# Edits in the opening of an attention and SwiGLU kernel: fill-in matmuls, a first fetch in halves, later stores, tied casts, and Down's scale noted later

## The chip, the cores and the metric

One core of a Trainium2 chip. The metric is the device time of one execution in microseconds (us), the median of several runs; lower is better. Engines are named as in the profile: PE is TensorE's matmuls and PEld its weight loads, DVE is VectorE, ACT is ScalarE, POOL is GpSimd, and SP is SyncE, which issues the DMAs in this kernel.

## The reference

For x of 2048 tokens by 512 features, xn is x normalized per token (layernorm without gain). The result is x + A(xn) * silu(B(xn)):

```
A: q, k, v = split(xn @ wqkv)            # 32 heads of 16
   p = softmax(where(0 <= i - j < 256, q k^T / 4, -1e9))
   A(xn) = (p v) @ wo
B: h = silu(xn @ w1) * (xn @ w3)         # 1792 wide
   B(xn) = h @ w2
```

## The kernel before

The tokens are worked in four tiles of 512, numbered t = 0 to 3. The FFN's width is cut in 14 blocks of 128. The large matmuls run in fp16: each operand is a high half and a low half (lo = value - hi), and a product is three matmuls of 512 columns, xh·wh, xh·wl and xl·wh, summed in PSUM. Weights are scaled by powers of two before they are cut in halves, and the scales are found on the chip: squares of each row (L249 on ACT, L251 on DVE), a cast of the sums to bf16 (L261, tile `sb`), a matmul with ones on PE (`powers`, L280 and L285), a short chain on DVE that makes the scale (L291 to L304), and then the cut (`split`: high half L333 on ACT, low half L334 on DVE; `split_pool`: L342 and L343 on ACT, L345 on POOL). In tile 0 the kernel does all this to the weights while it computes, and stores the cut weights in DRAM; tiles 1 to 3 load them from there.

The four pairs of columns of wqkv for q and k are called qk0 to qk3, one for each group of 8 heads; their raw halves are loaded at L395. `project` (L597, result read by L614 on ACT and L618 on DVE) computes q or k of a head group, `value` (L567, L570) computes v. Cut k and q of a group are stored in DRAM by L621 to L625, and `fetch` (L641) loads them back in the layout of the scores: `KA` the keys, `qa` the queries. Attention runs in two passes: scores for the row maxima (L665 on PE, L679 on DVE), then scores again, mask (L753), exponential (L756 on ACT) and values (L774).

`gate_up` (L1036) makes gate and up of a block, each in one bank: tanh of gate on ACT (L1051), times gate on DVE (L1055), times up on DVE (L1060), then the cut of h (L1069 on ACT, L339 on POOL). `measure(f)` finds the scales of blocks f and f + 1 of w1 and w3 and cuts them. `measure_down(k)` does it for groups of blocks of w2 (squares L923, cast L927), with the scale of the group in L935 to L945: `q` is the group's maximum, `dsc` what Down's result is multiplied with (L938), `fq` the running maximum over groups (L940, L942), `sw` the scale of the blocks (L945). Down is L1261 (and L1179 in folded form from tile 2 on), the output L1313 with its stores in L1324.

PSUM has two banks that alternate (`bank`, named m0 and m1 and shown as m), two tiles of two banks for scores (`scores_bank`, shown as s) and one (po) for scores and values. Matmuls that want bank m wait until the engine that reads its last content is done. SBUF has 54 slots, handed out by `take` and given back by `give(tile, after=n)`, n steps later.

PE runs its instructions in the order of the program text, which a planner for scores (`spread`, `more`, `beside_scores`) writes out. On the other engines a scheduler orders the instructions when the program is built, by readiness and priority; `tc.issue_after(ins)` keeps an instruction behind another of the same engine. `later(n, f)` runs f n steps further on in the program, where a step is one call of `step`, about once per piece of PE work. `lasts["emptied"]` is the last DVE instruction that read a bank of m.

In the opening, `keep_busy(n)` (L1534 to L1537) issues n matmuls of ones, whose results nobody reads, into a bank: 24 at the start, then 3, then 4 ahead of the first projections.

Of the kernel before, what the change touches and what calls it, by code (L numbers as in the profile page):

```python
# [10 lines left out]
F32 = mybir.dt.float32  # L11
# [4 lines left out]
ALU = mybir.AluOpType  # L16
# [5 lines left out]
P = 128  # L22
# [61 lines left out]
def tile_block(ctx: ExitStack, tc: tile.TileContext, x, wqkv, wo, w1, w3, w2, out):  # L84
# [59 lines left out]
    def later(n, f):  # L144
        made_so_far[0] += 1
        queue.append((now[0] + n, made_so_far[0], f))
# [16 lines left out]
    def bank(shape, dtype=F32):  # L163

        open_bank[0] = b = 1 - open_bank[0]
        return psm.tile(shape, dtype, name=f"m{b}", tag=f"m{b}", bufs=1)
# [414 lines left out]
    def project(t, g, k, terms=(range(3),), scores_bank=False):  # L581
# [7 lines left out]
        def part(n):  # L589
# [1 line left out]
            w = WQ[t, g, k]  # L591
            xh, xl = X[t]
            if n == 0:
                cell["pp"] = pss.tile([P, 2, TW], F32, name="s")[:, 0, :] if scores_bank else bank([P, TW])
            for c, i in parts[n]:
                a, b = ((0, xh), (1, xh), (0, xl))[i]
                nc.tensor.matmul(cell["pp"], w[:, (a * NC + c) * P:(a * NC + c + 1) * P], b[:, c, :], start=(c, i) == parts[0][0],  # L597
# [33 lines left out]
        WQ[t, g, k] = w = take(F16)  # L631
        nc.sync.dma_start(w, dWQ[g, k])

    def fetch(t, g):
        QA[t, g] = qa = qpool.tile([P, 4, TW], F16, name="qa")
        ka = keys(t, g)
        c0 = 0 if t else 2 * P
        for dst, d in ((ka[:, :, c0:], dK[g][:, :, t * TW - 2 * P + c0:(t + 1) * TW]),
                       (qa, dQ[g][:, :, t * TW:(t + 1) * TW])):
            for r in range(2):  # L640
                lasts["load"] = nc.sync.dma_start(dst[64 * r:64 * r + KR],  # L641
                                  d[64 * r:64 * r + 64].rearrange("(a d) i t -> (d i) a t", d=DH))

# [224 lines left out]

    measured = set()

    def measure(f, apart=0):

        raws = [RAW.pop(f + i) for i in range(2)]
        sb = squares([raws[0][0], raws[1][0], raws[0][1], raws[1][1]], on_act=4 if f > 2 else 2, apart=apart)

        def scale(s=None):
            pp = small.tile([P, 2, 2], F32, name="pp")
            pi = small.tile([P, 2, 2], F32, name="pi")  # L880
            return then(s, powers(sb, 4, pp.rearrange("p a b -> p (a b)"), pi.rearrange("p a b -> p (a b)"), s),
                        lambda: rest(pp, pi))

        def rest(pp, pi):
            ff = slice(f, f + 2)
            nc.vector.tensor_scalar(sg_scale[:, ff], pp[:, 0, :], 0.5 / (WS * XS), None, op0=ALU.mult)
            nc.vector.tensor_mul(p13[:, ff], pp[:, 0, :], pp[:, 1, :])
            measured.update((f, f + 1))

            def cut(i, k):  # L890
                if k == 0:
                    WF[0, f + i] = [[None, None], WF.pop((0, f + i), [None, None])[1]]
                WF[0, f + i][0][k] = a = take(F16)
                split_pool(a[:, 0:D], a[:, D:], raws[i][k], pi[:, k, i:i + 1])
                give(raws[i][k], after=5)
            for i in range(2):
                for k in range(2):
                    later(((1, 2, 4, 6) if f < 8 else (1, 5, 9, 13))[2 * i + k], lambda i=i, k=k: cut(i, k))
        if started:
            beside_scores(8, scale)  # L900
        else:
            later(10 if apart else 6, scale)

# [11 lines left out]
    def measure_down(k, f):  # L915
# [17 lines left out]
        def rest(p2):  # L933
# [1 line left out]
            nc.vector.tensor_mul(p2, p2, p13[:, f0:f1])  # L935
            q = small.tile([P, 1], F32, name="q")
            nc.vector.tensor_reduce(q, p2, axis=AX.X, op=ALU.max)
            nc.vector.tensor_scalar(down_scale[:, k:k + 1], q, 1.0 / (HS * WS), None, op0=ALU.mult)  # L938
            if k:
                nc.vector.tensor_max(fold_q, fold_q, q)  # L940
            else:
                nc.vector.tensor_copy(fold_q, q)  # L942
            nc.vector.reciprocal(q, q)
            sw = small.tile([P, 4], F32, name="sw2")
            nc.vector.tensor_scalar(sw[:, 0:n], p13[:, f0:f1], q, WS, op0=ALU.mult, op1=ALU.mult)  # L945

            def cut(f):
                raw = RAW2.pop(f)
# [344 lines left out]
    def total(t, b):  # L1293
# [4 lines left out]
        def part(half):  # L1298
# [16 lines left out]
            if half:  # L1315
# [10 lines left out]
                if t == NT - 1:  # L1326
                    store()
                else:
                    later(4, store)
                if b == 3:  # L1330
                    give(*(OT[t, g] for g in range(NG)))
        return opening([(6, lambda h=h: part(h)) for h in range(2)])
# [22 lines left out]
    def feed_forward():  # L1355
# [4 lines left out]
        for t in range(NT):  # L1360
            for f in range(FB):
                if t == 0:
# [3 lines left out]
                    elif f + LEAD == FB - 1:  # L1366
                        pieces += [(0, lambda f=f: load(0, f)) for f in range(FB - 2, FB)]
                    if f % 2 and f + 3 < FB:
                        pieces.append((0, lambda f=f + 3: later(5, lambda: measure(f, 1)) if f == 6 else measure(f, 1)))
                    pieces += [(0, lambda f=f: load_down(0, f)) for f in range(f + 2 if f else 0, min(f + 3, FB))]  # L1370
                    for m in range(f + 1 if f else 0, min(f + 2, FB)):
                        k = next(k for k, (_, f1) in enumerate(GROUPS) if m < f1)
# [158 lines left out]
        nc.gpsimd.memset(KA[2][:, a, :].bitcast(F32), TWO_ONES)  # L1531


    def keep_busy(n):  # L1534
        ps = bank([P, 4, P])
        for _ in range(n):
            nc.tensor.matmul(ps, onesb, onesb.unsqueeze(1).to_broadcast([P, 4, P]), start=True, stop=True)  # L1537

# [19 lines left out]
        flush()  # L1558
    with tc.issue_after(lasts["hi"].ins), tc.issue_after(lasts["x"].ins):
        qk[1][1]()  # L1560
    keep_busy(4)


    k00, q00 = (project(0, 0, k, ((0,), (1,), (2,)), k) for k in (1, 0))
    run([k00[0], q00[0], k00[1]])
    qk[1][2]()
    with tc.issue_after(lasts["scale"].ins):
# [2 lines left out]
    qk[1][3]()  # L1570
    with tc.issue_after(lasts["hi"].ins):
        run([k00[2], q00[2]])
    later(1, lambda: fetch(0, 0))
    k01 = project(0, 1, 1, ((0, 2), (1,)))
    run(k01[:1])
    wv[2]()
# [4 lines left out]
    sc["o"] = scaled(SQ["wv"][3], OS / WS, "so")  # L1581
    with tc.issue_after(lasts["hi"].ins):
        measure(0)
    run(project(0, 1, 0, scores_bank=True))
    later(1, lambda: fetch(0, 1))
    run(value(0, True))
    qk[2][1]()
# [35 lines left out]
    for n, u in enumerate(units):  # L1623
# [7 lines left out]
            wout[0]()  # L1631
        if n == 7:
            wout[1](2)
            beside_scores(12, lambda s: then(s, wout[2](s), lambda: later(2, lambda: wout[3](2)), lambda: later(3, out_scale)))
        want += a_unit - other[n]
        mine = more(want)

# [39 lines left out]
```

## Time and profile before

| quantity | before |
|---|---|
| median of 3 runs | 811.76 us (811.22 to 811.85) |
| profiled execution | 811.24 us |
| its span | 809.4 us |
| PE busy | 793.7 us (98%) |
| DVE, ACT, POOL busy | 631.2, 392.1, 377.1 us |
| granted TensorE clock | full in all 40 slices |

The profile covers one execution. Its page gives the busy time of each engine and the chain of work that ended last. In a timeline a row is the start, the duration, engine, line and operation, output and input tiles and the number of instructions put together; what stands in brackets is the idle time of that engine just before, and whose work ended it. A row with no bracket followed its predecessor with little or no idle time. Matmuls overlap: one of 512 columns is listed with 0.38 us, but in a row of them they start 0.216 us apart. 1.8 us of the profiled execution lie outside the span.

### The profile page before, as it was taken

To read this page: it belongs to the slowest core of one execution; us is meant where nothing else is said; L and a number is where in the kernel's file an instruction comes from. 1 tells how busy PE (TensorE), PEld (TensorE's weight loads), DVE (VectorE), ACT (ScalarE), POOL (GpSimd) and SP (SyncE) were. 2 spreads that over 40 slices of the span, in tenths; PEclk is the share of its full clock that TensorE was granted. 3 is DMA by queue.
4 is the path that set the end of the run, shared out by engine and by line. 5 is a ranking of instruction groups with operands and counts; after the bars stand their busy time and mean duration, and the time that the engine had idled before them with its cause. 6 is when DMAs were issued, how large, how long until landed. Compare 5 with 4: busy or idle time off the path is not lost.

```text
span 809.4 us, 23944 instructions
## 1 busy us (share of the span) xinstructions
PE 793.7 (98%) x9176; PEld 403.7 (50%) x9176; DVE 631.2 (78%) x2037; ACT 392.1 (48%) x591; POOL 377.1 (47%) x732
## 2 busy tenths in 40 slices
PE   8999989999999999999999999999999999999998
PEld 4444444444444444444444454456544754466465
DVE  8788788887888777887988888777778787875437
ACT  6879586553546544345344433344444234344411
POOL 2345376342329445354353455530346276550670
PEclk9999999999999999999999999999999999999999
DMA  9968554835576474757655634646372644335321
GB/s 282 265 214 267 160 183 134 278 114 191 160 199 208 134 232 139 218 142 263 160 162 181 194 104 119 185 137 179 105 201 74 160 139 137 113 90 172 111 65 62
DMA packets 109795, 134.19 MB, mean 166 GB/s; under 512 B 18864, under 2 KB 64880, under 8 KB 109680
## 3 DMA queue, kind: packets, MB, share of 16 engines
q1 hardware_dynamic: 109392, 132.13, 54.6%
q8 instruction: 72, 1.18, 0.6%
q10 hardware_dynamic: 288, 0.52, 0.2%
q14 instruction: 43, 0.35, 0.1%
HBM read 91.23 MB, written 36.57 MB: 158 GB/s over the span
## 4 chain that ended last, share of the span: by engine, by line
PE 79%; DVE 8%; ACT 6%; DMA 3%; issue 2%; SPq 1%; POOL 0%; ACTq 0%; DVEq 0%
PE m L1036 30%; PE po L774 8%; PE m L1261 8%; PE m L1179 8%; PE m L597 7%; PE s L746 5%; PE m L1313 4%; PE m L567 4%; PE s L665 3%; DMA slot<-in_B_w_dram 2%; DVE junk L679 2%; PE po L665 2%; ACT slot L342 1%; ACT pt L756 1%; ACT sqa L249 1%
## 5 line engine op out<-in xcount | busy, mean ns | idle before, releaser
L1036 PE MATMUL m<-XH,slot 128*128 128x512 f16 x896 | 267.4, 380 | 1.6 <-DVE slot L618 1.2
L756 ACT ACTIVATE pt<-s,es 128x1024 f32<-128x1024 f32 x152 | 167.5, 1112 | 193.7 <-DVE s L753 186.5
L1036 PEld LDWEIGHTS <-slot 128*128 128x128 f16 x1344 | 124.7, 98 | 156.0 <-issue 12.0
L1036 PE MATMUL m<-XL,slot 128*128 128x512 f16 x448 | 169.9, 379 | 0.0
L753 DVE TENSOR_TENSOR s<-s,MK 128x256 f32<-128x256 f32 (+2 forms) x280 | 118.7, 434 | 51.2 <-PE s L746 47.0
L679 DVE CUSTOM_DVE_ANT_0 junk<-s,MW 128x320 bf16<-128x320 f32 x276 | 133.9, 485 | 17.9 <-PE s L665 10.3
L339 POOL TENSOR_TENSOR slot<-slot,slot 128x256 f16<-128x256 f32 (+1 forms) x86 | 57.7, 692 | 141.9 <-ACT slot L1069 76.7
L345 POOL TENSOR_TENSOR slot<-slot,slot 128x128 f16<-128x128 f32 x168 | 69.1, 446 | 58.3 <-ACT slot L343 58.3
L679 DVE CUSTOM_DVE_ANT_0 junk<-po,MW 128x320 bf16<-128x320 f32 x172 | 83.4, 485 | 4.7 <-DVE mt L704 0.3
L1261 PE MATMUL m<-slot,slot 128*128 128x512 f16 x336 | 78.6, 380 | 0.3 <-DVE slot L1055 0.3
L774 PE MATMUL po<-pt,V 64*32 64x320 f32 (+4 forms) x2880 | 77.2, 342 | 0.8 <-DVE pp L304 0.8
L597 PE MATMUL m<-XH,slot 128*128 128x512 f16 x240 | 71.0, 380 | 1.6 <-DVE slot L1055 1.2
L1179 PE MATMUL m<-slot,slot 128*128 128x256 f16 x588 | 68.4, 273 | 0.0
L1094 POOL TENSOR_TENSOR slot<-slot,slot 128x256 f16<-128x256 f32 x98 | 64.6, 671 | 1.1
L1051 ACT ACTIVATE slot<-m,sgs 128x512 f32<-128x512 f32 x56 | 38.3, 683 | 54.4 <-PE m L1036 52.3
L774 PEld LDWEIGHTS po<-pt,V 64*32 64x32 f32 x2880 | 50.5, 106 | 22.9 <-PE s L515 0.9
L1179 PEld LDWEIGHTS <-slot 128*128 128x128 f16 x588 | 56.1, 98 | 11.5 <-issue 3.0
L1055 DVE SCALAR_TENSOR_TENSOR slot<-slot,m 128x512 f32<-128x512 f32 x56 | 38.3, 684 | 29.0 <-ACT slot L1051 29.0
L746 PE MATMUL s<-qa,KA 50*64 50x320 f16 (+3 forms) x1472 | 58.4, 260 | 0.1
L597 PEld LDWEIGHTS <-slot 128*128 128x128 f16 x384 | 35.6, 98 | 44.8 <-issue 3.4
L746 PEld LDWEIGHTS <-KA 50*64 50x64 f16 x1472 | 30.1, 106 | 51.9 <-issue 30.9
L1261 PEld LDWEIGHTS <-slot 128*128 128x128 f16 x336 | 30.7, 98 | 38.6 <-issue 4.2
(189 smaller groups left out, 1138.5 us busy)
## 6 DMA issues: line engine op xcount, KB each, us to landing
slot<-dW SPq DMA_DIRECT2D x98, 256.0 KB
slot<-in_B_w_dram SPq DMA_DIRECT2D x56, 256.0 KB
slot<-dFold SPq DMA_DIRECT2D x48, 256.0 KB
dW<-slot SPq DMA_DIRECT2D x42, 256.0 KB
slot<-in_A_x_dram SPq DMA_DIRECT2D x30, 256.0 KB
KA<-dK SPq DMA_DIRECT2D x24, 288.0 KB
qa<-dQ SPq DMA_DIRECT2D x32, 192.0 KB
slot<-dWQ SPq DMA_DIRECT2D x24, 256.0 KB
```

The costliest lines, as they stand in the source:

```text
L339: op(out[:, c], a[:, c], b[:, c])
L345: nc.gpsimd.tensor_sub(lo[:, c:c + P], raw[:, c:c + P], hi[:, c:c + P])
L597: nc.tensor.matmul(cell["pp"], w[:, (a * NC + c) * P:(a * NC + c + 1) * P], b[:, c, :], start=(c, i) == parts[0][0], stop=(c, i) == parts[ ...
L679: lasts["maximum"] = nc.vector.tensor_tensor_reduce(out=junk[:, :n], in0=s[:, r, :n], in1=mask, scale=1.0, scalar=NEG, op0=ALU.add, op1=AL ...
L746: nc.tensor.matmul(s[64 * h:64 * h + 64, r, o:o + 64 * n], ka[rows, 2 * p + a, 64 * (m + 4):64 * (m + 5)], qa[rows, 2 * p + a, 64 * (m + k ...
L753: nc.vector.tensor_add(v, v, MK[:, kind, of:of + n, :].unsqueeze(1).to_broadcast([P, 2 * len(which), n, 64]))
L756: lasts["exp"] = nc.scalar.activation(pt, s, AF.Exp, scale=es)
L774: nc.tensor.matmul(cell["po"][32 * i:32 * i + 32, h, 64 * (m + k):64 * (m + k + n)], V[64 * h:64 * h + 64, (4 * t + m // 2) % VB, hd * VW: ...
L1036: nc.tensor.matmul(cell[k], w[:, (a * NC + c) * P:(a * NC + c + 1) * P], b[:, c, :], start=c == 0 and i == 0, stop=c == NC - 1 and i == 2)
L1094: nc.gpsimd.tensor_sub(lo, view, hi)
L1179: nc.tensor.matmul(cell["ps"][:, c], made[:, f:f + P], wj[:, g:g + 256], start=j == j0 and c == 0 and n == 0, stop=j == j1 - 1 and n == 2, ...
L1261: nc.tensor.matmul(ps, hh[:, a * TW + b * P:a * TW + (b + 1) * P], w[:, c * D:(c + 1) * D], start=f == f0 and i == 0, stop=f == f1 - 1 and ...
```

## The change

1. In the opening, the fill-in matmuls ahead of the first projections are 3 instead of 4, and go to a scores tile, which the first projection of k then uses. The first projection of q uses a bank. `project` takes a function for the scores tile.
2. The first fetch (tile 0, group 0) is split by pairs of heads: four transfers for the first pairs, then four for the second, each of half the size.
3. `measure(6, 1)` is begun 8 steps later instead of 5, and its scale is set beside the scores of 6 rather than 8.
4. The cuts of blocks 8 to 13 come at steps 1, 4, 13 and 16 instead of 1, 5, 9 and 13, each with an `issue_after` on `emptied`.
5. In `measure_down` the reciprocal of q goes to a tile of its own, `iq`; `dsc` and `fq` are made in `note`, two steps later, with an `issue_after` on `emptied`.
6. The stores of the output of tiles 0 to 2 come 10 steps after their sum instead of 4.
7. The powers of wo are placed beside scores with 14 instead of 12.

```diff
-                cell["pp"] = pss.tile([P, 2, TW], F32, name="s")[:, 0, :] if scores_bank else bank([P, TW])
+                cell["pp"] = bank([P, TW]) if scores_bank is False else scores_bank()[:, 0, :]
...
-    def fetch(t, g):
+    def fetch(t, g, ps=None):
...
-        for dst, d in ((ka[:, :, c0:], dK[g][:, :, t * TW - 2 * P + c0:(t + 1) * TW]),
-                       (qa, dQ[g][:, :, t * TW:(t + 1) * TW])):
-            for r in range(2):
-                lasts["load"] = nc.sync.dma_start(dst[64 * r:64 * r + KR],
-                                  d[64 * r:64 * r + 64].rearrange("(a d) i t -> (d i) a t", d=DH))
+        for heads in (slice(0, 4),) if ps is None else [slice(2 * p, 2 * p + 2) for p in ps]:
+            for dst, d in ((ka[:, heads, c0:], dK[g][:, :, t * TW - 2 * P + c0:(t + 1) * TW]),
+                           (qa[:, heads, :], dQ[g][:, :, t * TW:(t + 1) * TW])):
+                for r in range(2):
+                    rows = slice(64 * r + DH * heads.start, 64 * r + DH * heads.stop)
+                    lasts["load"] = nc.sync.dma_start(dst[64 * r:64 * r + KR],
+                                      d[rows].rearrange("(a d) i t -> (d i) a t", d=DH))
...
+            def tied(i, k):
+                with tc.issue_after(lasts["emptied"].ins):
+                    cut(i, k)
...
-                    later(((1, 2, 4, 6) if f < 8 else (1, 5, 9, 13))[2 * i + k], lambda i=i, k=k: cut(i, k))
+                    if f < 8:
+                        later((1, 2, 4, 6)[2 * i + k], lambda i=i, k=k: cut(i, k))
+                    else:
+                        later((1, 4, 13, 16)[2 * i + k], lambda i=i, k=k: tied(i, k))
         if started:
-            beside_scores(8, scale)
+            beside_scores(until, scale)
...
-            nc.vector.tensor_scalar(down_scale[:, k:k + 1], q, 1.0 / (HS * WS), None, op0=ALU.mult)
-            if k:
-                nc.vector.tensor_max(fold_q, fold_q, q)
-            else:
-                nc.vector.tensor_copy(fold_q, q)
-            nc.vector.reciprocal(q, q)
+            iq = small.tile([P, 1], F32, name="iq")
+            nc.vector.reciprocal(iq, q)
             sw = small.tile([P, 4], F32, name="sw2")
-            nc.vector.tensor_scalar(sw[:, 0:n], p13[:, f0:f1], q, WS, op0=ALU.mult, op1=ALU.mult)
+            nc.vector.tensor_scalar(sw[:, 0:n], p13[:, f0:f1], iq, WS, op0=ALU.mult, op1=ALU.mult)
+
+            def note():
+                with tc.issue_after(lasts["emptied"].ins):
+                    nc.vector.tensor_scalar(down_scale[:, k:k + 1], q, 1.0 / (HS * WS), None, op0=ALU.mult)
+                    if k:
+                        nc.vector.tensor_max(fold_q, fold_q, q)
+                    else:
+                        nc.vector.tensor_copy(fold_q, q)
+            later(2, note)
...
-                    later(4, store)
+                    later(10, store)
...
-                        pieces.append((0, lambda f=f + 3: later(5, lambda: measure(f, 1)) if f == 6 else measure(f, 1)))
+                        pieces.append((0, lambda f=f + 3: later(8, lambda: measure(f, 1, 6)) if f == 6 else measure(f, 1)))
...
-    def keep_busy(n):
-        ps = bank([P, 4, P])
+    def keep_busy(n, ps=None):
+        ps = bank([P, 4, P]) if ps is None else ps
...
-    keep_busy(4)
...
-    k00, q00 = (project(0, 0, k, ((0,), (1,), (2,)), k) for k in (1, 0))
+    waiting = scores_bank()
+    keep_busy(3, waiting[:, 0, :].rearrange("p (k q) -> p k q", q=P))
...
+    k00, q00 = (project(0, 0, k, ((0,), (1,), (2,)), (lambda: waiting) if k else False) for k in (1, 0))
...
-    later(1, lambda: fetch(0, 0))
+    later(1, lambda: fetch(0, 0, (0, 1)))
...
-            beside_scores(12, lambda s: then(s, wout[2](s), lambda: later(2, lambda: wout[3](2)), lambda: later(3, out_scale)))
+            beside_scores(14, lambda s: then(s, wout[2](s), lambda: later(2, lambda: wout[3](2)), lambda: later(3, out_scale)))
```

What the scheduler makes of it shows at three places. The first is DVE in tile 0, at the maxima of the first scores. L261 128x2 is the cast of the sums of squares of qk3's first two quarters, the rows around it are maxima (L679 before, L681 after) and the scale of qk2. Before:

```order
L679 ISA junk,M<-s,M_106 128x256
L679 ISA M 128x1
L294 TENSOR_SCALAR al<-s 128x1
L261 CAST sb<-ssq 128x2
L679 ISA junk,M<-s,MW 128x320
```

And of the change, where lines 1055 of before are 1068:

```order
L334 SCALAR_TENSOR_TENSOR slot_726<-slot_205,sw_643,slot_726 128x512
L1068 SCALAR_TENSOR_TENSOR slot_737<-slot_737,m_716 128x512
L681 ISA junk,M<-s,MW 128x320
L681 ISA M 128x1
L261 CAST sb<-ssq 128x2
```

The cast has moved from ahead of four maxima and the rest of qk2's scale to behind them, behind the low halves of qk2 (L334) and behind the product of the first gate. At the same place on ACT, one of the two squares of qk3 that ran ahead of the second L570 now runs behind the tanh of the first gate, and two squares of w2 that ran behind that tanh now run behind the cast of the first h (L1069).

The second place is SP from the stores of the first k and q to the second fetch. Before (L395 are the two loads of qk3, dK_147, dQ_143, KA_140 belong to group 0 and the others to group 1):

```order
L625 DMA dK_147<-slot_408 128x512
L621 DMA dQ_143<-slot_417 128x2x512
L624 DMA dK_147<-slot_408 128x2x512
L622 DMA dQ_143<-slot_417 128x512
L395 DMA slot_551<-in_A_wqkv_dram 128x4x128
L625 DMA dK_148<-slot_462 128x512
L641 DMA KA_140<-dK_147 48x4x512 x2
L641 DMA qa<-dQ_143 48x4x512 x2
L624 DMA dK_148<-slot_462 128x2x512
L621 DMA dQ_144<-slot_495 128x2x512
L622 DMA dQ_144<-slot_495 128x512
L395 DMA slot_552<-in_A_wqkv_dram 128x4x128
```

And of the change, where the fetch is L643:

```order
L625 DMA dK_148<-slot_464 128x512
L643 DMA KA_140<-dK_147 48x2x512 x2
L643 DMA qa<-dQ_143 48x2x512 x2
L643 DMA KA_140<-dK_147 48x2x512 x2
L643 DMA qa<-dQ_143 48x2x512 x2
L624 DMA dK_148<-slot_464 128x2x512
L621 DMA dQ_144<-slot_497 128x2x512
L622 DMA dQ_144<-slot_497 128x512
L395 DMA slot_553<-in_A_wqkv_dram 128x4x128
L643 DMA KA_141<-dK_148 48x4x512 x2
L643 DMA qa<-dQ_144 48x4x512 x2
L395 DMA slot_554<-in_A_wqkv_dram 128x4x128
```

The first load of qk3 has moved from ahead of the first fetch to behind the stores of group 1, the second from ahead of the second fetch to behind it, and eight transfers stand where four stood.

The third place is DVE in the second group of Down's scales. Before:

```order
L935 TENSOR_TENSOR pp_1851<-pp_1851,p_156 128x4
L937 TENSOR_REDUCE q<-pp_1851 128x1
L938 TENSOR_SCALAR dsc<-q 128x1
L940 TENSOR_TENSOR fq<-fq,q 128x1
L943 RECIPROCAL q<-q 128x1
L945 TENSOR_SCALAR sw_1924<-p_156,q 128x4
```

And of the change, where L935 to L945 are L943 to L955:

```order
L943 TENSOR_TENSOR pp_1854<-pp_1854,p_156 128x4
L945 TENSOR_REDUCE q<-pp_1854 128x1
L947 RECIPROCAL iq<-q 128x1
L953 TENSOR_SCALAR dsc<-q 128x1
L955 TENSOR_TENSOR fq<-fq,q 128x1
L949 TENSOR_SCALAR sw_1933<-p_156,iq 128x4
```

The reciprocal has moved ahead of `dsc` and `fq`; these two still stand ahead of `sw`. The third group reads alike; in the first group they stand behind `sw` and one L1055. On PE, one matmul of the fill-in is gone, the tiles of the opening have other names, and one group of 16 matmuls of the powers of wo (L285) has changed places with one turn of 8 matmuls (L515) near 225 us; the rest of PE's order is the same. On ACT the order over the cuts of blocks 8 to 13 is the same, too.

4 lines of the change are left out of this document (2 added, 2 removed).

## The prediction

> **What bounds the kernel now.** I read the page first (shares, then the chain that ended last), then the busy time by stretches, then every idle gap of TensorE (PE) in its timeline, and last what VectorE (DVE), ScalarE (ACT) and the DMA issuer SyncE (SP) do just ahead of those gaps.
>
> ```profile
> span 809.4 us, 23944 instructions
> PE 793.7 (98%) x9176; PEld 403.7 (50%) x9176; DVE 631.2 (78%) x2037; ACT 392.1 (48%) x591; POOL 377.1 (47%) x732
> ...
> PE 79%; DVE 8%; ACT 6%; DMA 3%; issue 2%; SPq 1%; POOL 0%; ACTq 0%; DVEq 0%
> ```
>
> PE is busy in 98% of the span, and 79% of the chain is PE itself: PE's own work cannot shrink here (the change takes one matmul away), so only the 15.7 us in which PE stands still can. The stretches say where those are; the columns are PE, PEld, DVE, ACT and POOL busy.
>
> ```profile
> 10.00:20.00 10.00, 9.10 (x51) 5.05 (x52) 8.95 (x25) 8.26 (x18) 0.00 (x0) 1.00 1.12 295
> 50.00:60.00 10.00, 8.97 (x58) 3.84 (x51) 8.79 (x36) 7.88 (x18) 6.70 (x14) 1.00 0.62 195
> 60.00:70.00 10.00, 10.00 (x80) 4.44 (x78) 8.34 (x38) 9.02 (x16) 5.93 (x14) 1.00 0.87 281
> 70.00:80.00 10.00, 8.70 (x68) 3.79 (x68) 8.77 (x27) 9.90 (x23) 4.93 (x8) 1.00 0.80 254
> 110.00:120.00 10.00, 7.19 (x95) 3.57 (x94) 8.22 (x33) 8.41 (x16) 8.13 (x19) 1.00 0.42 121
> 170.00:750.00 580.00, 579.54 (x7159) 296.43 (x7158) 458.67 (x1447) 250.94 (x329) 265.95 (x474) 1.00 0.54 159
> ```
>
> Between 170 and 750 us PE is idle for 0.46 us in all: nothing that moves there can gain, it can only lose. Everything that the change can win lies in the first 130 us, in these gaps of PE (at the end of a row: idle time before it, and who released it):
>
> ```profile
> 12.85 1.02 PE L1537 MATMUL m<-onesb 128*128 128x512 bf16 x4 [0.58 <-DVE XL L501]
> ...
> 30.15 0.30 PE L665 MATMUL s<-KA,qa 48*64 48x128 f16 x7 [0.41 <-DMA qa<-dQ]
> ...
> 42.29 0.59 PE L1036 MATMUL m<-XH,slot 128*128 128x512 f16 x2
> ...
> 55.33 0.59 PE L1036 MATMUL m<-XH,slot 128*128 128x512 f16 x2 [1.03 <-DVE slot L618]
> ...
> 76.93 0.33 PE L665 MATMUL po<-KA,qa 48*64 48x320 f16 x4 [0.84 <-DVE M L679]
> ...
> 115.04 0.59 PE L597 MATMUL m<-XH,slot 128*128 128x512 f16 x2 [1.19 <-DVE slot L1055]
> ...
> 118.47 0.30 PE L665 MATMUL s<-KA,qa 48*64 48x256 f16 x4 [1.62 <-ACT pt L756]
> ```
>
> **The change, part by part.** The sum runs along PE: by how much it is ahead of before at each of these gaps.
>
> *Fill-in matmuls.* Before, they write a bank of m and wait for DVE to read it (L501); the last transposes had started at 11.78.
>
> ```profile
> 11.78 0.49 PE L493 MATMUL s<-identf,slot 128*128 128x128 f32 x3
> 12.41 0.62 ACT L496 CAST XH<-s 128x512 f16<-128x512 f32 x1
> 13.71 1.03 PE L597 MATMUL s<-XH,slot 128*128 128x512 f16 x4
> 15.67 0.16 DVE L261 CAST sb<-ssq 128x2 bf16<-128x2 f32 x1
> 16.30 0.19 PE L280 MATMUL s<-sb,onesb 128*128 128x1 bf16 x2
> ```
>
> In a free s tile they start when the transposes end (12.27), and three at the 0.22 us spacing of a 512-column matmul end at 12.9. The projection behind them then waits only for the last XH, at 12.41 + 0.62 = 13.03, and begins at about 13.1 instead of 13.71: 0.6 us ahead. The cover of the next 3 us decides how much stays. The powers matmul at 16.30 needs the cast that ends at 15.83, which hangs on ACT's squares and not on PE; PE, 0.6 ahead, would be there at 15.7 and starts at about 15.9. 0.4 stays.
>
> *Fetch in halves, and qk3's load behind it.* PE's wait at 30.15 is for qa of the first head group.
>
> ```profile
> 22.49 0.43 SPq L395 DMA_DIRECT2D slot<-in_A_wqkv_dram  x1
> ...
> 24.48 0.82 SPq L641 DMA_DIRECT2D KA<-dK  x2
> 25.39 0.88 SPq L641 DMA_DIRECT2D qa<-dQ  x2
> ```
>
> The last of the four transfers is issued at 25.8 and lands just ahead of 30.15, 4.3 us later, with the 256 KB weight load and 768 KB of the fetch itself in the queues. At the 267 GB/s moved between 20 and 30 us, halving what is asked for first takes 384 KB or 1.4 us out of the way, and the moved load about 1 us. PE needs it 0.4 + 0.41 = 0.8 us earlier. The 0.41 goes: 0.8 ahead. The price is four more issues on SP, each 0.41 to 0.44 us by these rows, so 1.7 us, which delay the second fetch (issued from 30.87, first read by PE near 40), the first loads of w1 and w3 behind it, and qk3's second load.
>
> The page "DMA: Bandwidth & Descriptors" of the Trainium skill (Anatomy of one DMA) speaks against this part: it puts a transfer at about 2.0 us fixed plus its bytes at 436 GB/s, on another issuing path than SP's. By that, half of 192 KB saves an estimated 0.2 us, half of the wait stays, and the sum would be 0.2 smaller. The row of 4.3 us is far from the 2.4 us that this gives for a whole transfer; here it is the queue that takes the time.
>
> *The cast of qk3's squares.* DVE takes its instructions in order, and stood 1.60 us before this cast, though everything behind it was ready:
>
> ```profile
> 37.47 0.17 DVE L261 CAST sb<-ssq 128x2 bf16<-128x2 f32 x1 [1.60 <-ACT sqa L249]
> 39.28 0.15 DVE L302 TENSOR_SCALAR sw<-al 128x1 int32<-128x1 int32 x1
> 41.56 0.68 DVE L1055 SCALAR_TENSOR_TENSOR slot<-slot,m 128x512 f32<-128x512 f32 x1
> 44.27 0.69 DVE L1060 SCALAR_TENSOR_TENSOR slot<-m,slot 128x512 f32<-128x512 f32 x1
> ...
> 54.59 0.69 DVE L618 SCALAR_TENSOR_TENSOR slot<-m,slot 128x512 f16<-128x512 f32 x1
> ```
>
> ```profile
> 39.47 1.34 ACT L333 ACTIVATE slot<-slot,sw 128x512 f16<-128x512 f32 x2 [1.45 <-DVE sw L302]
> 40.71 0.67 ACT L1051 ACTIVATE slot<-m,sgs 128x512 f32<-128x512 f32 x1
> 44.99 0.62 ACT L1069 CAST slot<-slot 128x512 f16<-128x512 f32 x1 [2.25 <-DVE slot L1060]
> 53.65 0.58 ACT L614 ACTIVATE slot<-m 128x512 f16<-128x512 f32 x1
> ```
>
> In the new order the cast stands behind L1055. Without the stall (1.60), the cast itself (0.17) and a reordering of a maximum (about 0.5), the scale L302 comes about 2.3 us earlier, near 37.0; ACT follows with L333, and L1051 at 38.5 (the gate it reads is ready at 38.1 by PE's lead). L1055 frees PE's bank at 39.8. Before, it ended at 42.24, and PE started at 42.29, 0.2 us after its previous matmul; that goes too: 1.0 ahead. From L1069 on ACT works without a break until 57, in the old order and in the new, so its start at 42.7 instead of 44.99 is carried along. I add the new order's ACT instructions between L1069 and the second L614 at the spacing that these forms have before (casts 0.51, squares and scales 0.62, the first L614 0.47): the second L614 starts at 51.4 instead of 53.65. L618 ended 1.63 us after that start before, which is 53.0 now. PE, 1.0 ahead, arrives at 53.1, so the 1.03 goes: 2.0 ahead. This is the largest term, and one with little slack: from some 0.1 us on, whatever makes ACT later costs as much.
>
> Between 57 and 77 PE is led by the same two engines (ACT is busy in 9.02 and 9.90 us of 10), so it keeps the lead that they have, which I take as 1.85 (DVE's 2.3 at L302, less 0.45 where its maxima now stand ahead of the next scale). The wait of 0.84 at 76.93 is one in their order and keeps its size: 1.85 ahead at 77.
>
> *Down's scale and the running maximum.* The chain behind PE's two largest gaps, on DVE and ACT:
>
> ```profile
> 113.03 0.16 DVE L937 TENSOR_REDUCE q<-pp 128x1 f32<-128x4 f32 x1
> ...
> 113.30 0.15 DVE L940 TENSOR_TENSOR fq<-fq,q 128x1 f32<-128x1 f32 x1
> 113.48 0.16 DVE L943 RECIPROCAL q<-q 128x1 f32<-128x1 f32 x1
> 113.68 0.72 DVE L945 TENSOR_SCALAR sw<-p,q 128x4 f32<-128x4 f32 x1
> 114.32 0.68 DVE L1055 SCALAR_TENSOR_TENSOR slot<-slot,m 128x512 f32<-128x512 f32 x1
> ```
>
> ```profile
> 114.44 1.33 ACT L342 ACTIVATE slot<-slot,sw 128x512 f32<-128x512 f32 x2 [1.23 <-DVE sw L945]
> ...
> 117.33 1.09 ACT L756 ACTIVATE pt<-s,es 128x1024 f32<-128x1024 f32 x1
> ```
>
> "Two steps later" would take the scale and the maximum out of this chain; in the order of the second group they still stand ahead of sw. What changes is that the reciprocal, in a tile of its own, goes ahead of them. It then starts where the scale did (113.22), the other two follow 0.08 apart while it runs, and sw starts near 113.46: 0.2 us less, for PE at 115.04 and, by way of ACT's exponential at 117.33, at 118.47. The first group saves a little more at 64 us, where DVE waits 1.33 us for ACT afterwards: nothing. 2.05 ahead at 120.
>
> *The rest, at nothing.* The casts of blocks 8 to 13 are tied to a DVE instruction, but run on ACT and POOL: ACT's order over those blocks is the same in both. Squares of blocks 6 and 7, the powers of wo and the later stores act after 80 us beside a PE without gaps; what covers them is the 0.46 us of idle in 580. If that cover goes, each costs what it makes PE wait, which no row shows; I bound it between 0 and the slower rival below. The other side is 0.46: more cannot be gained there. The remaining gaps, at 124.50 and later, hang on work that the change leaves alone.
>
> Sum: 0.4 + 0.4 + 0.2 + 1.0 − 0.15 + 0.2 = 2.05 us. From the profiled execution's 811.24 us that leaves 809.2. That execution lies 0.52 under the median of the runs shown, 811.76, so the forecast of the median is **809.7 us**.
>
> **Rivals.**
>
> *The gain is swallowed by ACT's backlog.* ACT's work is not less, only ordered otherwise: squares of qk3 and w2 that filled its idle time at 41 to 43 now stand between L1069 and the second L614. Should they (or a load that they wait for) hold L614 at its old place less PE's early lead, only the prologue's terms survive, 0.8, and 0.2 at 114: 1.0 or less, 810.8. For it: ACT is at 9.9 of 10 at 70 to 80. Against it: ACT stood idle for 2.25 us ahead of L1069, while the two squares that move behind it take 1.2.
>
> *Slower: a store that stays longer holds a slot.* The output stores are issued six steps later, so the slot with the totals is free later, and an instruction of another kind that is given this slot waits for the store to land. If such an instruction is L1055, PE's next bank waits behind it. A transfer here took 4.3 us from issue to landing, and PE has one group of 12 matmuls of 0.216 us, 2.6 us, in hand: 1.7 us lost each time. Nothing in the stretch of 170 to 750 could give it back. It decides from two such waits that fall into a landing (3.4 − 2.05 = 1.35: 813.1) and ends clearly slower with three (814.8). For it: PE has no reserve there, and such a wait on a transfer stands at one L1055 of the new order. Against it: stores wait long on SP already before, without PE waiting for a transfer anywhere after 30.15.
>
> *The squares of qk3 come late.* Its second load is issued near 33.2 and its square, in ACT's order ahead of L1069, is due near 39.0. At the 4.3 us seen above it lands at 37.5. From 5.8 us on, each us later takes one from the 2.0. The prologue would keep 0.8 and the reciprocal 0.2, so this ends between 809.7 and 810.8, at the first rival's price at worst.
>
> *The change does not do what it says* where it ties casts and moves Down's scale; that is in my sum already. If, beyond it, the reciprocal gains nothing, the forecast moves by 0.2 to 809.9.
>
> **Numbers.** A measurement of this kernel can tell about 0.2% from no change, 1.6 us: faster means under 810.1, slower over 813.4. My forecast (with the last rival) 0.54; swallowed or late squares 0.27, most of it between 810.2 and 811.4; a wait for stores 0.19, of which 0.16 above 813.4. A small part of the forecast's share lies above 810.1. So: faster 0.53, same 0.31, slower 0.16. Below, the end is the sum with half of the waits at 76.93 and 115.04 gone besides: 809.7 − 0.42 − 0.6 = 808.7. Above, the range takes in the swallowed case and the first part of the slower one, 813.0.
>
> **What would show it.** In the profile after: the projection L597 at 13.1; no DMA wait at 29.3; no idle before a cast L261 128x2 near 36; L1069 near 42.7; PE's wait before L1036 near 53 under 0.2; sw 0.4 us after the reduction at 111; PE idle under 0.6 us between 170 and 750. A second L614 later than 52.5, or a wait for a transfer on PE or L1055 after 170 us, would make the prediction wrong.

## The result, and the profile after

The changed kernel takes 815.4 us (814.2 to 816.83, 5 runs) against 811.56 before: ratio 1.005, 95% interval [1.0036, 1.0064]. It is slower by 3.8 us, where 2.05 less was forecast.

The profile after is of the execution of 816.83 us. Page, then two windows of it (PE, PEld, DVE, ACT, POOL busy, then the granted clock), and the second window before:

```profile
span 815.0 us, 23978 instructions
...
PE 796.0 (98%) x9175; PEld 406.0 (50%) x9175; DVE 636.4 (78%) x2037; ACT 392.1 (48%) x591; POOL 378.5 (46%) x732
```

```profile
10.00:20.00 10.00, 9.38 (x46) 5.81 (x46) 7.99 (x22) 8.09 (x17) 0.00 (x0) 0.83 1.15 298
250.00:270.00 20.00, 15.95 (x180) 7.63 (x185) 16.22 (x43) 13.10 (x22) 15.25 (x32) 1.00 0.48 145
```

```profile
250.00:270.00 20.00, 19.99 (x267) 9.58 (x266) 16.85 (x53) 10.52 (x16) 17.75 (x34) 1.00 0.46 142
```

The second window is the loss: PE is busy for 15.95 us of the 20, before for 19.99. PE's gaps in the timeline show it, and the four in the middle did not exist before:

```profile
55.27 0.59 PE L1049 MATMUL m<-XH,slot 128*128 128x512 f16 x2 [0.63 <-DVE slot L618]
...
119.00 0.30 PE L667 MATMUL s<-KA,qa 48*64 48x256 f16 x4 [1.63 <-ACT pt L758]
...
260.15 0.42 PE L748 MATMUL s<-qa,KA 50*64 50x320 f16 x12 [0.87 <-ACT pt L758]
...
261.04 0.42 PE L748 MATMUL s<-qa,KA 50*64 50x320 f16 x12 [0.47 <-DVE XL L525]
...
266.34 0.59 PE L1049 MATMUL m<-XH,slot 128*128 128x512 f16 x2 [1.87 <-DVE slot L1068]
...
268.96 0.33 PE L667 MATMUL s<-KA,qa 48*32 48x320 f16 x8 [0.74 <-ACT pt L758]
...
756.21 0.59 PE L1049 MATMUL m<-XH,slot 128*128 128x512 f16 x2 [0.37 <-DVE slot L1068]
```

By position: 0.06 ahead of before at 55 us, 0.53 behind at 119, 5.34 behind at 756 (the same gap stood at 750.87 before). The four gaps are 3.95 of that. The 0.53 behind at 119 arise just before, half of it at scores at 112 us and half at PE's wait that ends at 115.58, which is 1.46 us here and was 1.19; ahead of it the maximum `fq` took 0.65 us instead of 0.15. Of the profiles below with the new order of Down's scale, experiment 3's has the same 0.65 and 1.46, those of 1, 4, 5, 7 and 14 have 0.41 and 1.18. Why they differ is open, and so is a new wait of 0.38 at 534. The first window holds a chance of its own: PE's clock fell while it stood between the fill-in matmuls and the transposes at 9 to 10.6 us, ahead of all changed instructions of PE; eight transposes that took 1.08 us before took 1.75, and the projections began at 14.72. So in this execution the opening's gain cannot be seen; the runs below show it.

Around the four gaps, DVE in the changed kernel, then the last three of these instructions before, and PE's next group there that wants the bank that L1055 reads:

```profile
257.86 0.69 DVE L618 SCALAR_TENSOR_TENSOR slot<-m,slot 128x512 f16<-128x512 f32 x1 [1.30 <-ACT slot L614]
...
261.31 4.06 DVE L824 TENSOR_SCALAR dr<-dr,so 128x32 f32<-128x32 f32 x1
265.28 0.42 DVE L755 TENSOR_TENSOR s<-s,MK 128x256 f32<-128x256 f32 x1
265.61 0.67 DVE L1068 SCALAR_TENSOR_TENSOR slot<-slot,m 128x512 f32<-128x512 f32 x1
```

```profile
259.62 0.52 DVE L822 TENSOR_SCALAR dr<-dr,so 128x32 f32<-128x32 f32 x1
260.05 0.42 DVE L753 TENSOR_TENSOR s<-s,MK 128x256 f32<-128x256 f32 x1
260.38 0.67 DVE L1055 SCALAR_TENSOR_TENSOR slot<-slot,m 128x512 f32<-128x512 f32 x1
```

```profile
262.63 0.59 PE L1036 MATMUL m<-XH,slot 128*128 128x512 f16 x2
```

A scaling of 32 columns, 0.23 to 0.86 us at its fifteen other places in this execution, took 4.06. Behind it stand the mask that the exponential needs and L1068, which frees PE's bank. POOL at that time:

```profile
251.88 6.21 POOL L345 TENSOR_TENSOR slot<-slot,slot 128x128 f16<-128x128 f32 x16 [2.68 <-ACT slot L343]
...
260.34 0.71 POOL L1007 TENSOR_TENSOR slot<-slot,slot 128x256 f32<-128x256 f32 x1
...
264.94 0.39 POOL L1019 CAST slot<-slot 128x256 f16<-128x256 f32 x1
265.40 0.67 POOL L1020 TENSOR_TENSOR slot<-slot,slot 128x256 f16<-128x256 f32 x1
```

POOL works without a pause from 251.88, the 16 low halves of wo first, to 265.33; the scaling ends at 265.37. A run of POOL without a pause is not new, though, and does not hold DVE by itself: before, POOL was busy for more of this window (17.75 us against 15.25), and in its unbroken run from 241.55 to 255.65 this small DVE instruction took a third of a microsecond:

```profile
246.76 0.34 DVE L691 TENSOR_SCALAR NM<-M 128x16 f16<-128x16 f32 x1
```

On ACT the cuts of wo have moved, too, from an idle stretch to one ahead of the exponentials (after, then before):

```profile
249.39 1.33 ACT L342 ACTIVATE slot<-slot,swwo 128x512 f32<-128x512 f32 x2 [0.24 <-DVE swwo L302]
...
257.24 0.58 ACT L614 ACTIVATE slot<-m 128x512 f16<-128x512 f32 x1
258.98 1.11 ACT L758 ACTIVATE pt<-s,es 128x1024 f32<-128x1024 f32 x1 [1.16 <-DVE s L755]
```

```profile
241.23 0.72 ACT L342 ACTIVATE slot<-slot,swwo 128x512 f32<-128x512 f32 x1
...
255.49 0.60 ACT L614 ACTIVATE slot<-m 128x512 f16<-128x512 f32 x1 [0.16 <-PE m L597]
257.30 1.11 ACT L756 ACTIVATE pt<-s,es 128x1024 f32<-128x1024 f32 x1 [1.22 <-DVE s L753]
```

ACT runs without a break from 249.39 until L614 has read its bank; before, L614 had to wait for PE. So theory A: part 7 of the change, "14 instead of 12", makes the loss, by two mechanisms: ACT's cuts, late and in front of L614 and the exponential, and POOL's run, beside which one DVE instruction is now held until it ends. Theory B, the rival on record: the stores, or one of the moved squares.

### The profile page after: what moved, and what is told of

The parts are those of the page before. It is cut to its first block, busy times and chain, and to the rows that moved or that the text cites. A ratio compares the mean times of both kernels' runs of the same rounds, so it can differ in the third digit from the quotient of the medians.

```text
span 815.0 us, 23978 instructions
## 1 busy us (share of the span) xinstructions
PE 796.0 (98%) x9175; PEld 406.0 (50%) x9175; DVE 636.4 (78%) x2037; ACT 392.1 (48%) x591; POOL 378.5 (46%) x732
## 3 DMA queue, kind: packets, MB, share of 16 engines
q8 instruction: 72, 1.18, 0.6%
## 5 line engine op out<-in xcount | busy, mean ns | idle before, releaser
L681 DVE CUSTOM_DVE_ANT_0 junk<-s,MW 128x320 bf16<-128x320 f32 x276 | 134.1, 486 | 17.3 <-PE s L667 9.4
L681 DVE CUSTOM_DVE_ANT_0 junk<-po,MW 128x320 bf16<-128x320 f32 x172 | 83.5, 485 | 4.6 <-DVE al L298 0.4
L1068 DVE SCALAR_TENSOR_TENSOR slot<-slot,m 128x512 f32<-128x512 f32 x56 | 38.3, 685 | 28.7 <-ACT slot L1064 26.6
```

Of the source, the lines that this page charges most:

```text
L681: lasts["maximum"] = nc.vector.tensor_tensor_reduce(out=junk[:, :n], in0=s[:, r, :n], in1=mask, scale=1.0, scalar=NEG, op0=ALU.add, op1=AL ...
```

## The experiments

**1. The change with wo's powers put back.** `- beside_scores(14, ...)  + beside_scores(12, ...)`

> The changed kernel with one part undone: the powers of wo beside scores with 12 again. Theory A (the place of wo's powers): PE's four waits between 260 and 269 us (0.87 + 0.47 + 1.87 + 0.74 = 3.95 us) go, the time is 811.2 to 811.7. Within A there are two mechanisms, told apart by other runs: POOL's longer unbroken run of work, beside which one DVE instruction (the scaling of dr by so) takes 4.06 us instead of 0.52, or ACT's cuts of wo, which come 9 us later and stand ahead of the exponential. Theory B (the stores that are held longer, or the moved squares, make the waits): the waits stay, 815 +- 0.5.

Measured: 810.88 us (12 runs, 810.02 to 818.67) against 811.51, ratio 1.0001 [0.9985, 1.0018]. The loss is gone: A, not B. (The four gaps are missing from the profile as well, but PE comes 7 us late there for another reason, so it is the median that tells.) The profile, which fell on the execution of 818.67, shows two things more. The opening without a fall of the clock:

```profile
13.09 1.02 PE L597 MATMUL s<-XH,slot 128*128 128x512 f16 x4 [0.16 <-ACT XH L496]
...
54.00 0.59 PE L1049 MATMUL m<-XH,slot 128*128 128x512 f16 x2 [0.99 <-DVE slot L618]
...
117.15 0.30 PE L667 MATMUL s<-KA,qa 48*64 48x256 f16 x4 [1.63 <-ACT pt L758]
```

PE is 1.33 us ahead at 54 and 1.32 at 117. And a hold of another instruction (DVE), with what it does to PE:

```profile
245.58 7.79 DVE L693 TENSOR_SCALAR NM<-M 128x16 f16<-128x16 f32 x1
```

```profile
255.17 0.64 PE L748 MATMUL s<-qa,KA 50*64 50x320 f16 x8 [5.53 <-ACT pt L758]
...
257.82 1.06 PE L1049 MATMUL m<-XH,slot 128*128 128x512 f16 x2
258.68 0.63 PE L1049 MATMUL m<-XL,slot 128*128 128x512 f16 x1
...
260.37 0.60 PE L597 MATMUL m<-XH,slot 128*128 128x512 f16 x2
260.80 0.38 PE L597 MATMUL m<-XL,slot 128*128 128x512 f16 x1
```

Here, too, POOL's run (without a pause from 239.91 to 253.33) and the held instruction (253.37) end together. L693 is L691 of the kernel before. PE stands 5.53 us and then runs at half its rate until 260.4, three matmuls in 1.28 us instead of 0.65. The Trainium skill's "TensorE: Matmul & The Clock Gate" (Part 1: The HAM clock gate) says that the clock halves after an idle window of about 3.4 us; this stand agrees. Shorter ones have no single outcome: gaps up to 1.87 us left the clock at 1.00 in the change's window, while in experiment 5 the clock falls after stands of 1.41 and 0.47.

**2. The kernel before, with the move of wo's powers alone.** `- beside_scores(12, ...)  + beside_scores(14, ...)`

> The kernel before with only the powers of wo moved from 12 to 14. Theory A: this alone makes the loss, the scaling of dr near 260 us takes about 4 us and the time is 815 to 816. Theory B: no loss, 811.6 +- 0.5.

Measured: 816.42 us (4 runs, 816.38 to 816.61), ratio 1.0059 [1.0045, 1.0074]. This one number of the change costs 4.9 us, and the hold is there:

```profile
261.60 4.05 DVE L822 TENSOR_SCALAR dr<-dr,so 128x32 f32<-128x32 f32 x1
```


**3. The scaling with two tensors.** `- tensor_scalar(dr, dr, so, ...)  + scalar_tensor_tensor(dr, dr, so, dr, mult, bypass)`

> The changed kernel, with the scaling of dr by so in another form: a tensor_scalar with one tensor from SBUF becomes a scalar_tensor_tensor with dr as a second, ignored tensor. If DVE's one-tensor form waits for a pause of POOL, this form should wait at most for the POOL instruction that runs (fq's maximum took 0.65 beside POOL, at 113.65): the 4.06 us shrink to under 1, the waits of 1.87 and 0.74 go, and 812.5 to 813.2 is left, with the waits of 0.87 and 0.47 that ACT's cuts make. If it is something else than POOL that holds this instruction (its place behind another, or its scalar), it stays at 4 us and 815.4.

Measured: 815.64 us, 1.0051 [1.0038, 1.0064]. The form does not matter; POOL's run ends at 263.53 here, and this at 263.58:

```profile
259.51 4.07 DVE L824 SCALAR_TENSOR_TENSOR dr<-dr,so 128x32 f32<-128x32 f32 x1
```

**4. Down's scale alone** (part 5 on the kernel before).

> The kernel before with only the new order of Down's scale. As the prediction has it: the scale sw of the second group comes 0.2 us earlier after the reduction, 811.3. By the profile of the change: the maximum fq, now at a moment when POOL has just begun an instruction, takes 0.65 us instead of 0.15, and PE's wait behind it grows by 0.3: 811.6 to 812.0, unless POOL's work falls otherwise here.

Measured: 811.69 us, 1.0002 [0.9993, 1.0011]; PE's wait at 115.05 is 1.18, as before. No 0.2 us, and no loss.

**5. The scaling on ACT.** `- nc.vector.tensor_scalar(dr, dr, so, ...)  + nc.scalar.activation(dr, dr, AF.Copy, scale=so)`

> The changed kernel, with the scaling of dr by so done by ACT instead of DVE. The form with two inputs was held for 4.07 us as well, so what is left of theory A's two mechanisms is tested by taking the instruction off DVE. Hold beside POOL: PE's waits of 1.87 (L1068) and 0.74 (exponential) near 266 to 269 go, 812.6 to 813.2; what remains of the loss are the waits of 0.87 and 0.47 made by ACT's cuts of wo. If the place of ACT's cuts alone made all of it, 815.4 stays. A third outcome is that the next DVE instruction that touches only SBUF is held in its stead: then the wait moves and the time stays.

Measured: 812.86 us (10 runs), 1.0017 [1.0008, 1.0026]: 2.5 us back of the change's 815.4, as expected from 1.87 + 0.74. What is left are the two gaps ahead of it:

```profile
258.57 0.42 PE L748 MATMUL s<-qa,KA 50*64 50x320 f16 x12 [1.41 <-ACT pt L758]
259.46 0.42 PE L748 MATMUL s<-qa,KA 50*64 50x320 f16 x12 [0.47 <-DVE XL L525]
```

The hold is so priced at 2.5 us. About 2.0 us are left between 812.86 and experiment 1, for which ACT's cuts are the cause by their place, ahead of L614 and the exponential; no run moves ACT's cuts alone. This profile, of the execution of 813.77, does not give that price either: PE loses 3.6 us at this place, 1.41 + 0.47 in the two gaps and the rest by its clock, which fell just behind them:

```profile
260.08:263.49 3.41, 3.41 (x12) 1.20 (x9) 2.47 (x9) 2.32 (x3) 3.41 (x8) 0.50 0.85 245
```

In how many of the ten executions (811.65 to 815.23) the clock fell is not known.

**6. The opening alone** (parts 1 and 2 on the kernel before).

> The kernel before with the opening alone (three fill-in matmuls in a scores tile, first fetch in halves). The scheduler then moves the cast of qk3's squares as in the whole change. From the run with wo's powers put back: PE 0.6 ahead at 13.1, no wait for qa at 30, 1.3 ahead at 54 and at 165, where the prediction said 2.05. If nothing is lost behind 165 us: 810.2. If the shift gives some of it back later (another phase of POOL and DVE near 245 to 260): 810.5 to 811.3, with a wait of PE there.

Measured: 811.1 us (11 runs, two of them at 819.5 and 819.75), 1.0003 [0.9985, 1.0022]. In the profile:

```profile
13.20 1.02 PE L597 MATMUL s<-XH,slot 128*128 128x512 f16 x4 [0.17 <-ACT XH L496]
...
53.74 0.59 PE L1038 MATMUL m<-XH,slot 128*128 128x512 f16 x2 [0.62 <-DVE slot L618]
...
165.48 0.30 PE L667 MATMUL s<-KA,qa 48*64 48x256 f16 x4 [0.73 <-ACT pt L758]
```

No wait for qa near 30, 1.6 us ahead at 54, 1.7 at 165. The profiled execution is the one of 819.75, and it has the hold of L693 (7.79 us) again, the instruction that stood in such a run before without being held. That of 819.5 has no profile; by its time I take it for the same.

**7. Wo's powers put back, and the scaling on ACT** (1 and 5 together).

> The change without the move of wo's powers and with the scaling of dr on ACT. If the opening's 1.3 us stands: 810.2, below before (811.5). The place where one execution of the kernel without the move stood 5.5 us (a DVE instruction, L693, beside POOL at 245 to 253) is untouched, so single executions of 816 to 819 may still show.

Measured: 811.86 us (12 runs, 810.48 to 820.68), 1.0027 [1.0, 1.0053]. Not below before: three executions are at 819 to 820.7, and the profile of one has the hold of L693 again. Taking one instruction off DVE does not cure it. The nine others have a median of 811.73, so more than the hold is missing from the forecast of 810.2; what, is open.

**8. Parts 3, 4 and 6 alone** on the kernel before.

> The kernel before with parts 3, 4 and 6 alone: measure(6) later, the cuts of blocks 8 to 13 at other steps and tied, the stores 10 steps later. The prediction has these at nothing: 811.5 +- 0.5. The prediction's slower rival (a store that holds a slot, and an instruction that waits for it to land) would be 1.7 us or more slower, with a wait of PE after 170 us.

Measured: 811.6 us, 1.0005 [0.9996, 1.0013]. Nothing, as forecast; the rival of the stores falls.

**9. Trials of a hold, behind the kernel before.** For each trial POOL runs n subtractions of 256 or 128 columns and DVE one small instruction:

```
nc.gpsimd.tensor_sub(po, a, pd)                    # n times
nc.vector.tensor_scalar(e, d, ea, None, mult)      # or tensor_tensor, PSUM operand, reciprocal
```

> The kernel before, with trials behind its end (work that the reference doesn't ask for, so only the trials' durations count): ACT writes two tiles, POOL then runs 0, 1, 2, 4 or 8 subtractions without a pause, and DVE, some 0.3 us later, one small instruction (32 columns). The forms are a scaling of one SBUF tensor, a product of two SBUF tensors, a product with one operand from PSUM, and a reciprocal. Theory A (an unbroken POOL run holds it): the scaling takes 0.2 us alone, and with 1, 2, 4, 8 POOL instructions of 0.7 us it ends when POOL stops, so up to 5 us at 8; the product of two the same by the 4.07 us that the two-input form took; PSUM and reciprocal stay near 0.2. Rival (it waits for the one instruction that runs): never over 0.9 us, whatever the count.

Measured: scaling 0.52 to 0.68 beside POOL's 256 columns and 0.24 beside its 128; product of two 0.52 to 0.53 and 0.43, and 0.19 alone; PSUM operand 0.19 and reciprocal 0.35 beside 128 columns. None is held, as the rival says, but the trial is weaker than planned: DVE's trials ran ahead of POOL's, so each met one of the first runs, and POOL's subtractions waited for each other (eight took 6.33 us, in experiment 12 without pauses 5.50).

**10. The opening alone, with the folded weights' cuts spaced.** `- later(2 * n, ...)  + later(4 * n, ...)`

> The opening alone, with the four cuts of folded weights (POOL's work beside wo's low halves) 4 steps apart instead of 2, so that POOL pauses between them. If POOL's unbroken run makes the 5.5 us in single executions of the opening alone: no execution over 813, median 810 to 810.9. If the pauses don't matter, single executions of 816 to 820 come again.

Measured: 810.45 us (12 runs), 1.0003 [0.9981, 1.0024], but two executions at 817.56 and 819.59. The forecast of no execution over 813 fails. This says nothing on pauses, for the edit made none where they were wanted: in the profiled execution (810.06) POOL works without one from 239.62 to 253.73, around L693. That instruction is not held here:

```profile
245.28 0.35 DVE L693 TENSOR_SCALAR NM<-M 128x16 f16<-128x16 f32 x1
```


**11. The opening alone, with wo's powers earlier.** `- wout[1](2); beside_scores(12, ...)  + wout[1](1); beside_scores(7, ...)`

> The opening alone, with wo's squares one step apart instead of two and its powers beside scores with 7 instead of 12, so that POOL cuts wo mostly before the folded weights begin. Theory A: shorter common run, 810 to 810.9 and no execution over 813. If the place of wo's cuts is not what counts, as the opening alone: 811.1 with single executions of 816 to 820.

Measured: 810.68 us (11 runs, 810.46 to 811.14), 0.9988 [0.998, 0.9997], no execution over 811.2. Here POOL pauses at 246.03, 0.17 us after L693 has begun, so no long run lies beside it. Of the 1.76 us that PE is ahead at 165 it has 0.86 at 750. Most of the difference is lost at a load that came in time before and is late for it:

```profile
337.00 0.60 PE L597 MATMUL m<-XH,slot 128*128 128x512 f16 x2 [0.56 <-DMA slot<-dWQ]
```

**12. The trials in sequence, with POOL's instructions apart** (each writes a place of its own, so that none waits for the one before).

> The trials again behind the kernel before, now one after the other, with POOL's subtractions in two kinds: each writes what the one before wrote, so that it waits for its end (as in the first trials, a pause of about 0.1 us each), or each writes a place of its own, so that they follow without a pause, as the cuts of wo and of the folded weights do. If it is the missing pause that holds DVE: the scaling of one tensor takes 0.5 to 0.7 us in the first kind, and in the second until POOL's last instruction ends: about 5 us at 8 instructions of 0.69 us, 2.5 at 4, 10 at 16, 4.5 at 12 of 0.39. The product of two tensors from SBUF likewise. If not: 0.4 to 0.7 us in both kinds.

Measured: 0.62 to 0.63 beside 256 columns (once 0.41), 0.35 beside 128, in both kinds, also at 16 instructions in 10.95 us; once DVE came before POOL, 0.24. The expectation fails: a run without pause is not enough.

**13. The trials with the moment varied** (a product from PSUM of 32 columns more in each trial ahead of the scaling).

> The trials once more, behind the kernel before: eight POOL instructions without a pause (first 14 trials: 256 columns to float32; then 12 trials: 128 columns to fp16, as the low halves of wo), and DVE first runs a product from PSUM whose length grows by 32 columns from trial to trial, then the scaling of 32 columns. So the scaling begins at another moment of POOL's instruction in each trial, behind a busy DVE as in the kernel. If the moment decides who gets the port: in one or a few trials the scaling is held for the rest of the run (2 to 5 us), in the others 0.2 to 0.8. If never: none over 0.9, and what makes the long holds of 4.06 and 7.79 us stays open.

Measured, in all trials (27 in the run) at most 0.78. Three of them (DVE), and POOL's run of the last:

```profile
814.25 0.46 DVE L1676 TENSOR_SCALAR slot<-slot,slot 128x32 f32<-128x32 f32 x1
...
857.93 0.23 DVE L1676 TENSOR_SCALAR slot<-slot,slot 128x32 f32<-128x32 f32 x1
...
882.28 5.49 POOL L1674 TENSOR_TENSOR slot<-slot,slot 128x256 f32<-128x256 f32 x8 [0.72 <-ACT slot L1666]
882.94 0.78 DVE L1676 TENSOR_SCALAR slot<-slot,slot 128x32 f32<-128x32 f32 x1
```

A scaling that begins 0.30 us into POOL's instruction (0.69 long) waits for its end; 0.53 into it, not at all; 0.66 into it, for the next one. The moment sets the size, but within one instruction.

**14. The whole change, with wo's powers earlier instead of later** (the edit of 11, on the change).

> The whole change, but with the powers of wo earlier than before (7 instead of 14, squares one step apart) instead of later. From the opening alone with the same edit (810.68, no execution over 811.2) and the parts measured at nothing: 810.4 to 811, no execution over 813. If another DVE instruction falls into POOL's run in this combination: single or all executions of 813 or more.

Measured: 810.42 us (11 runs, 809.48 to 811.01), 0.9983 [0.9974, 0.9992]: 0.9 us below the kernel before (811.34) and 5.0 below the change, and no execution above 811.01. Executions of 817 us and more came 8 times in the 47 of experiments 1, 6, 7 and 10; were they as frequent in 11 and 14, their 22 executions would be free of them in about 2 cases of 100 (estimate). Five of the eleven lie at 809.48 to 809.75. The profiled one, 811.01, has the fall of the clock at 10 us again (its eight transposes take 1.69).

## Why the prediction was wrong

- **Fill-in matmuls, fetch in halves: right.** Projections at 13.09 where 13.1 stood, no wait for qa; in experiment 1 PE was 0.39, 0.77 and 0.95 us ahead where 0.4, 0.8 and 1.0 stood (at 16, 30 and 42 us). Where the clock falls at 10 us this is covered up.
- **The cast of qk3's squares: right in kind, too large.** In experiment 1 L302 came at 36.90 (37.0 forecast), L1068, the L1055 of before, ended at 40.45 (39.8), and L1082, the L1069 of before, came at 43.20 (42.7). But the second L614 came at 51.85, not 51.4, and L618 only at 53.26, behind two maxima in DVE's order, where I had carried its old distance from L614 along. The wait of 1.03 that should have gone was 0.99 in experiment 1 and 0.62 in 6. The lead at 165 us was 1.3 to 1.8 where the clock did not fall at 10 us and `fq` did not take 0.65, not 2.05. Of that, 0.5 to 1.0 us was left at the end, by the medians of experiments 1, 6 and 10 without their executions over 817, and nothing in 7.
- **Down's scale: wrong by its 0.2.** The two instructions that stayed ahead of `sw` took up what the reciprocal gained: `fq` took 0.41 us in experiment 4, 0.15 before.
- **"The rest, at nothing": the step that failed.** It was right for the squares, the tied casts and the stores (experiment 8) and wrong for the powers of wo: +4.9 us alone. The text covered them with "beside a PE without gaps". That PE has no gap tells nothing about how far ACT and DVE are ahead of it. At the place where the moved work lands, L1055 ended at 261.05 and PE's next matmul into its bank was due at 262.63: 1.6 us of slack, less than the 3.5 by which the scaling grew. And ACT's cuts were moved from an idle stretch into one where L614 and an exponential follow. The slack and ACT's rows were there to be read; the growth of the scaling was not, since no row of before shows a hold.
- **The slower rival** had the right sign for "PE has no reserve there" and the wrong mechanism; stores cost nothing. A rival for each moved part, by its queue, could have named ACT's cuts: the prediction read POOL only where DVE's own operations were short.

**What stays open.** That POOL holds the scaling is shown by the ends that agree within 0.05 us in all six holds that a profile shows, of 4.05 to 7.79 us, and that the hold costs 2.5 us by experiment 5. Why it lasts for the whole run there and for one POOL instruction in all trials, at 27 moments, with runs up to 16, is not settled. The trials differ in one thing from the holds: in unbroken runs DVE came at most 0.73 us after the run's start, in the holds 5.7 or 9.4 us after. But that does not decide either, since L693 of experiment 10 came 5.66 us after a run's start, with 8.4 us of it to go, and took 0.35. It began 0.107 us into POOL's instruction, and the same instruction in experiment 8, not held either (0.37), 0.089; the three held ones began 0.078 to 0.087 into it. Whether such hundredths count is not tested (the trials' moments lie 0.03 apart). Open is, too, why single executions of 1, 6 and 7, and by their times 10, have the hold and others don't. The Trainium skill's "SBUF — State Buffer" (Who interferes with whom) has DVE and GpSimd share one port pair as an exclusive lock, which whoever comes first keeps for the whole instruction. The trials agree (0.62 beside one that runs, no wait with an operand from PSUM); the long holds, over 8 to 18 of POOL's instructions, go beyond it.

## What to carry to other kernels

An engine that is never idle is no cover for work that is moved onto its suppliers: read, at the place itself, by how much the instruction that frees its next buffer comes ahead, and what the moved work queues in front of it on every engine, GpSimd included. Small DVE instructions on SBUF beside a long GpSimd run mostly cost tenths of a microsecond, but can cost several, by the times in every execution of one kernel (experiment 2) and in single ones of another (experiment 6), so long GpSimd runs belong where DVE's next instruction is not on the path; here the same work some steps earlier instead of later turned +3.8 us into −0.9. A gain at the start was worth less at the end than where it arose (1.76 and 0.86 us in experiment 11), in part because a load that was just in time became late.

## What the runs showed of the hardware

- A DVE instruction of 32 columns, 0.24 us alone, took 4.05 to 4.07 us beside GpSimd's work in three profiles, and one of 16 columns 7.78 to 7.79 in three others, each until GpSimd's next pause; in trials 0.62 beside one instruction of 256 columns and 0.35 beside one of 128. Two forms were held alike (4.06 and 4.07). The same instruction of 16 columns took 0.34 and 0.35 us beside as long a run in two other profiles.
- After 5.53 us without matmuls TensorE ran at half its rate for about 5 us (255.17 to 260.37, experiment 1). Shorter stands did it in some places: 1.41 and 0.47 us in experiment 5 (granted clock 0.50 for 3.41 us), and 1.34 and 0.57 between fill-in matmuls in the first 15 us of the change (eight transposes in 1.75 us instead of 1.08). In others they did not: 0.87, 0.47, 1.87 and 0.74 in the change's window at 250 to 270 (1.00).
